# Routing attention and a top-1 router: four 32-row mask products side by side, and the preparation pieces gathered at one place per turn

## The chip, the cores and the metric

The kernel runs on one core of a Trainium2 chip. The metric is the time of one execution on the device in microseconds (us); the figure for a kernel is the median of several runs. Engines are named as in the profile: PE is TensorE (matmuls and transposes; PEld its weight loads), DVE is VectorE, ACT is ScalarE, POOL is GpSimd, SP is SyncE, which issues most DMAs.

## The reference

Attention with routing by clusters, then a router that sends each token to one of eight experts. Sizes: 4 batches, 8 heads, 768 rows, head width 64, 16 clusters; 3072 tokens of width 512, expert width 1024.

```python
q_assign = np.argmax(np.einsum('bhsd,hcd->bhsc', q_n, c_n), axis=-1)
k_assign = np.argmax(np.einsum('bhsd,hcd->bhsc', k_n, c_n), axis=-1)
mask = q_assign[:, :, :, None] == k_assign[:, :, None, :]
scores = scale * np.matmul(q, k.transpose(0, 1, 3, 2))
scores = np.where(mask, scores, -1000000000.0)
scores = scores - np.max(scores, axis=-1, keepdims=True)
attn = np.exp(scores)
attn = attn / (np.sum(attn, axis=-1, keepdims=True) + 1e-09)
return np.matmul(attn, v).astype(np.float32)
...
logits = xn @ en.T / tau
expert_idx = np.argmax(logits, axis=1)
...
    h = np.maximum(x[mask] @ w1[e], 0.0)
    out[mask] = gate_w[mask, None] * (h @ w2[e])
```

The token rows `x` of the router are the attention's output, heads side by side.

## The kernel before, in words

**Stages.** Attention, then a short stage that sorts tokens by expert, then 28 blocks of 128 tokens through their expert. The change is in the attention alone.

**Units, turns, pairs, groups.** Two heads are worked on together (a head pair; 16 of them, four per batch). A pair has 12 units: two halves of the query rows (`hq`, 384 each) by six tiles of 128 keys (`j`). Six units are a group, which has one output bank `o_ps`. The main loop takes two units a turn, so a pair has six turns (0 to 5) and a group three. In a turn it issues the scores and exponentials of the next two units, then the attends of its own two: the loop is one turn ahead with the scores.

**A unit.** `scores` (L338): per head one mask product in bf16 (64 rows of `kH` by `qH`, which hold one-hot cluster numbers times 2^60 and a -1/1 column, so that pairs in different clusters end at a huge negative value), then per head the f32 product of `kT` and `qT`, accumulated in the same banks `s_ps` (two banks a unit, two units at a time). The two heads lie on rows 0 to 63 and 64 to 127 of the array. `expo` (L349): ACT takes the exponential into `prob` (five buffers). `attend`: PE multiplies `prob` with `v` into `o_ps` (L358), two heads on two column halves; DVE adds `prob` into the running sum `acc` (L367 for a group's first two units, L377 for the others).

**End of a group.** One turn later, in turns 0 and 3: `total` sums `acc` over the partitions on PE (L385) and ACT copies it to `den` (L393); `divide` takes the reciprocal on DVE (L401) and makes `xT` (L402), with `ev`, a tiny multiple of the sum of the values. `rows` transposes `xT` on PE (L419) and ACT copies it to `xr` (L424), in turns 2 and 5.

**Preparation of the next pair** is cut in pieces, and `prep()` takes the next one at two places of a turn: between the scores and the attends, and behind the attends (and `total`, `divide`). The pieces in order: `turn` transposes the first halves of q and k (L220; ACT copies q, L227, DVE copies k, L229), with `values`, which sums v on POOL (L291 to L293); `turn` of q's second half; of k's; `products` with the centroids on PE (L235, copied by ACT, L243); `assign` (PE transposes, L248; DVE finds each row's maximum, L256, and where it is, L257; POOL multiplies by a preference, L258, so that ties go to the first); `choose` (DVE: L264 the best preference `pm`, L265 the one-hot `oh`); an empty one; `turn_hot` of q (six bf16 transposes on PE, L277, copied by DVE, L283); of k (six more, copied by ACT, L285); `mean` (L298, L306), which makes `ev`.

**Routing of a batch** (`route_pieces`) runs in the turns after its last group, one piece a turn at the end of a turn: `products` with the expert embeddings (L441, copy L449), `logits` (L454, L457), `norms` (three squares on ACT, L467), and `choose` (some 12 small DVE operations, L478 to L493, with a square root and an exponential on ACT, each with a table load), then the rows are written to DRAM. For the last batch these pieces come one after the other behind the loop.

**Buffers.** PSUM: four banks for scores, two for outputs, and two (`psM`, taken by `misc()` in turn) for everything else: each use waits until the one two before it has been copied out.

**Order.** PE, DVE and ACT issue in the order of the program text. POOL and SP are ordered by a scheduler. Loads of q, k, v of the next pair are issued on SP at a pair's start in the text; the first expert weights behind the loads of pair 2.

The loop's place for a piece, before:

```python
piece = prepare.pop(0) if prepare else None
```

Of the kernel before, what the change touches and what calls it, by code (L numbers as in the profile page):

```python
# [35 lines left out]
def kernel(  # L36
# [67 lines left out]
    with ExitStack() as at:  # L104
# [15 lines left out]
        def load(n):  # L120
            b, hp = pairs[n]
            t = ld[n] = {}
            for nm, src in (("q", q), ("k", k), ("v", v)):
                t[nm] = ldp.tile([P, NJ, 2, D], F32, tag=nm + "32", name=nm + "32")
                for h in range(2):
                    nc.sync.dma_start(
                        out=t[nm][:, :, h],
                        in_=src[b, 2 * hp + h].rearrange("(p j) d -> p j d", j=NJ),
                    )
# [4 lines left out]
        load(0)  # L134
# [34 lines left out]
        ohs = [const.tile([P, NJ // 2, 4, 2, D], BF16, name=f"oh{i}") for i in range(2)]  # L169
        for oh in ohs:  # L170
            nc.gpsimd.memset(oh, 0.0)
            for t in range(2):
                nc.gpsimd.memset(oh[:, :, 2 * t : 2 * t + 2, :, C : C + 1], (-1.0, 1.0)[t])
# [35 lines left out]
        def prep_pieces(n):  # L209
# [21 lines left out]
            def products():  # L231
# [10 lines left out]
                t["asT"] = smp.tile([P, HS], F32, tag="asT", name="asT")  # L242
                nc.scalar.copy(t["asT"], bk[:, 0:HS])  # L243

            def assign():
                bk = misc()
                for u in range(NJ // 2):
                    nc.tensor.transpose(  # L248
                        bk[:, P * u : P * u + P], t["asT"][:, P * u : P * u + P], ident
                    )  # L250
# [3 lines left out]
                sel = smp.tile(shp, BF16, tag="sel", name="sel")  # L254
# [5 lines left out]
            def choose():  # L260

                shp = [P, 4 * NJ, C]
                pm = smp.tile(shp[0:2], BF16, tag="pm", name="pm")
                nc.vector.tensor_reduce(pm, t["sel"], axis=AXX, op=ALU.max)  # L264
                nc.vector.tensor_tensor(  # L265
                    oh.rearrange("p u t h c -> p (u t h) c")[:, :, 0:C],
                    t["sel"],
                    bc(pm, shp, 2),
                    ALU.is_equal,
                )  # L270

            def turn_hot(i, nm):
                hot = t[nm + "H"] = trp.tile([P, S], BF16, tag=nm + "H", name=nm + "H")
                bk = misc().bitcast(BF16)
                for j in range(NJ):
                    half, u = divmod(j, NJ // 2)
                    nc.tensor.transpose(  # L277
                        bk[:, P * j : P * j + P],
                        oh[:, u, 2 * i + half].rearrange("p h c -> p (h c)"),
                        identb,  # L280
                    )
                if nm == "q":
                    nc.vector.tensor_scalar(hot, bk[:, 0:S], BIG, None, ALU.mult)  # L283
                else:
                    nc.scalar.copy(hot, bk[:, 0:S])  # L285
# [10 lines left out]
            def mean():  # L296
                bk = misc()
                nc.tensor.matmul(  # L298
                    bk[:, 0:1],
# [6 lines left out]
                nc.vector.tensor_copy(t["ev"], bk[:, 0:1])  # L306


            return [
                lambda: (turn("q", 0), turn("k", 0), values()),  # L310
                lambda: turn("q", 1),
                lambda: turn("k", 1),
                products,
                assign,
                choose,
                None,
                lambda: turn_hot(0, "q"),
                lambda: turn_hot(1, "k"),
                mean,
            ]  # L320

# [8 lines left out]
        def scores(i):  # L330

            n, hq, j = units[i]
            t = ld[n]
            s_ps = un[i]["s_ps"] = psS.tile([P, 2, 512], F32, tag="s_ps", name="s_ps")
            for l, r, first in (("kH", "qH", True), ("kT", "qT", False)):
                for h in range(2):
                    rows = slice(D * h, D * h + D)
                    nc.tensor.matmul(  # L338
                        s_ps[:, h, 0:HS],
                        lhsT=t[l][rows, P * j : P * j + P],  # L340
                        rhs=t[r][rows, HS * hq : HS * hq + HS],
                        start=first,
                        stop=not first,
                    )
# [84 lines left out]
        def route_pieces(b):  # L429
# [4 lines left out]
            def products(half):  # L434
# [13 lines left out]
                t["pT"] = smp.tile([P, HS], F32, tag="asT", name="asT")  # L448
                nc.scalar.copy(t["pT"], bk[:, 0:HS])  # L449

            def logits(half):
                bk = misc()
                for u in range(U):
                    nc.tensor.transpose(  # L454
                        bk[:, P * u : P * u + P], t["pT"][:, P * u : P * u + P], ident
# [8 lines left out]
            def norms(half):  # L464
                for j in range(U * half, U * half + U):
                    junk = smp.tile([P, DM], F32, tag="junk", name="junk")
                    nc.scalar.activation(  # L467
                        junk, xr[b][:, j, 0:DM], ACTF.Square, accum_out=t["sq"][:, j : j + 1]
                    )

            def choose():
# [26 lines left out]

            return [
                lambda: products(0),  # L500
                lambda: (logits(0), norms(0)),
                lambda: products(1),
                lambda: (logits(1), norms(1)),
                choose,
            ]


        prepare, routing = [], []

        def prep():  # L510
            piece = prepare.pop(0) if prepare else None
            if piece:
                piece()

        with tc.manual_schedule(engines={EngineType.PE, EngineType.DVE, EngineType.Activation}):
            for piece in prep_pieces(0):
                if piece:
                    piece()
            for m in range(2):
                scores(m)  # L520
                expo(m)


            for i in range(0, len(units) + 6, 2):
                g, part = divmod(i, GU)
                if i < len(units) and i % (2 * NJ) == 0:
                    n = i // (2 * NJ)
                    assert not prepare
                    if n + 1 < len(pairs):
                        load(n + 1)  # L530
                        prepare = prep_pieces(n + 1)
                    if n == 1:

                        for w in range(2):
                            nc.sync.dma_start(
                                out=w1s[w], in_=moe_w1[0].rearrange("(c p) f -> p c f", p=P)
                            )
                            nc.sync.dma_start(
                                out=w2s[w], in_=moe_w2[0].rearrange("(c p) d -> p c d", p=P)
                            )  # L540
                for m in range(i + 2, min(i + 4, len(units))):
                    scores(m)
                    expo(m)
                prep()
                if part == 4 and g > 0:
                    rows(g - 1)
                for m in range(i, min(i + 2, len(units))):
                    attend(m)
                if part == 0 and g > 0:
                    total(g - 1)  # L550
                    divide(g - 1)
                prep()
                if routing:
                    routing.pop(0)()
                if part == 4 and g > 0 and g % (2 * NHP) == 0:
                    assert not routing
                    routing = route_pieces(g // (2 * NHP) - 1)
            for piece in routing:
# [251 lines left out]
```

## Time and profile before

| | |
|---|---|
| median of 3 runs | 904.12 us (903.97 to 904.96) |
| the profiled execution | 904.4 us, its span 902.4 us, mean PE clock 0.973 |
| PE busy | 842.1 us (93%) |
| DVE, ACT, POOL busy | 357.1, 301.6, 127.8 us |
| L338, products of q and k, f32, x768 | 156.3 us busy, 486 ns each |
| L338, masks, bf16, x384 | 63.9 us busy, 329 ns each |
| L358, attends, f32, x768 | 145.1 us busy, 499 ns each |
| L377, sums on DVE, x128 | 130.1 us busy, 1017 ns each |
| L401, reciprocals on DVE, x32 | 81.7 us busy, 2552 ns each |
| L277, one-hot transposes, x192 | 16.7 us busy, 226 ns each |
| L258, POOL's product, x16 | 24.3 us busy, 1516 ns each |

The timeline has start, duration, engine, line, operation, names, shapes, count, and in brackets the idle time before it and what ended it. The rows of a stretch have: from and to; its length; busy time and count of PE, PEld, DVE, ACT, POOL; PE's granted clock; the DMA engines' busy share; GB/s. PE's matmuls overlap: a record lasts longer than the time until the next one starts. An f32 product shows as two records. The slices of the page are 22.6 us each.

### The profile page before, as it was taken

What the parts mean: (1) busy time and instruction counts of PE and PEld (TensorE: products, weight loads), DVE (VectorE), ACT (ScalarE), POOL (GpSimd) and SP (SyncE); (2) the same over time, 40 slices, a digit from 0 to 9 for tenths busy, and PEclk for the clock granted to TensorE, in tenths of its full rate; (3) what the DMA queues carried; (4) which work ended last, traced back from release to release, by engine and by line L of the source; (5) the groups of instructions that cost most, each with busy time, mean ns of one, the idle gap of its engine ahead of it and who ended that gap; (6) DMA issues with size and microseconds to landing.
All of it is one profiled execution on the core that took longest, in us unless ns stands there. A gap on an engine that the chain in (4) does not pass through costs nothing.

```text
span 902.4 us, 12774 instructions
## 1 busy us (share of the span) xinstructions
PE 842.1 (93%) x5207; PEld 495.4 (55%) x5207; DVE 357.1 (40%) x488; ACT 301.6 (33%) x485; POOL 127.8 (14%) x171
## 2 busy tenths in 40 slices
PE   4999999999999999999628999999999999999996
PEld 2444444444444444444216777767676777767672
DVE  3577777877777877687750000000000000000000
ACT  3545556654566555755330111111111111111110
POOL 4011010211111111110021011110101010101010
PEclk8999999999999999999957999999999999999998
DMA  9822211322213122020011380756565656405610
GB/s 246 303 54 53 53 36 35 108 53 53 53 36 106 36 54 53 19 88 1 1 70 36 117 321 26 259 188 256 192 259 188 259 196 260 156 24 198 234 36 21
DMA packets 105645, 106.85 MB, mean 118 GB/s; under 512 B 77157, under 2 KB 77157, under 8 KB 105072
## 3 DMA queue, kind: packets, MB, share of 16 engines
q1 hardware_dynamic: 100928, 92.30, 31.8%
q0 software_dynamic: 4480, 13.65, 4.0%
q8 instruction: 43, 0.70, 0.3%
q14 instruction: 18, 0.15, 0.0%
q10 hardware_dynamic: 176, 0.05, 0.0%
HBM read 152.11 MB, written 13.64 MB: 184 GB/s over the span
## 4 chain that ended last, share of the span: by engine, by line
PE 38%; issue 28%; DMA 20%; DVE 9%; ACT 2%; POOL 1%; SPq 0%; POOLq 0%; DVEq 0%
DMA out_dram<-y,sidx 19%; PE s_ps L338 15%; PE o_ps L358 12%; DVE den L401 4%; PE misc L220 3%; PE misc L385 2%; PE misc L235 2%; PE misc L419 1%; DVE acc L377 1%; DVE xT L402 1%; ACT den L393 1%; PE misc L441 1%; PE misc L248 1%; DVE qH L283 1%; PE misc L298 1%
## 5 line engine op out<-in xcount | busy, mean ns | idle before, releaser
L714 PEld LDWEIGHTS h_ps<-xTm,w1s 128*128 128x128 f32 x1792 | 204.6, 193 | 22.1 <-DVE xTm L704 19.7
L714 PE MATMUL h_ps<-xTm,w1s 128*128 128x128 f32 x1792 | 208.7, 278 | 2.9 <-DMA w1s<-in_moe_w_dram 2.9
L727 PE MATMUL y_ps<-w2s,hT 128*128 128x512 f32 x448 | 201.2, 592 | 0.0
L349 ACT ACTIVATE prob<-s_ps 128x768 f32<-128x768 f32 x192 | 153.2, 811 | 100.2 <-PE s_ps L338 78.0
L704 DVE COPY xTm<-x_ps 128x512 f32<-128x512 f32 x28 | 19.4, 691 | 380.9 <-PE x_ps L702 380.9
L338 PE MATMUL s_ps<-qT,kT 64*128 64x384 f32 x768 | 156.3, 486 | 0.0
L358 PE MATMUL o_ps<-prob,v 128*64 128x384 f32 x768 | 145.1, 499 | 0.0
L377 DVE TENSOR_TENSOR acc<-acc,prob 128x768 f32<-128x768 f32 x128 | 130.1, 1017 | 4.9
L727 PEld LDWEIGHTS y_ps<-w2s,hT 128*128 128x128 f32 x448 | 81.0, 190 | 81.3 <-issue 81.3
L721 ACT ACTIVATE hT<-h_ps 128x512 f32<-128x512 f32 x56 | 33.4, 597 | 243.7 <-PE h_ps L714 243.7
L401 DVE RECIPROCAL den<-den 128x384 f32<-128x384 f32 x32 | 81.7, 2552 | 30.8 <-ACT den L393 30.8
L338 PEld LDWEIGHTS s_ps<-qT,kT 64*128 64x128 f32 x768 | 69.3, 190 | 21.3 <-issue 21.3
L736 POOL DMA_INDIRECT out_dram<-y,sidx x28 | 28.5, 1017 | 356.1 <-ACT y L735 350.2
L358 PEld LDWEIGHTS o_ps<-prob,v 128*64 128x64 f32 x768 | 46.5, 136 | 56.7 <-issue 55.1
L338 PE MATMUL s_ps<-qH,kH 64*128 64x384 bf16 x384 | 63.9, 329 | 1.6 <-ACT prob L349 1.3
L735 ACT ACTIVATE y<-y_ps,xin 128x512 f32<-128x512 f32 x28 | 19.2, 687 | 136.1 <-PE y_ps L727 129.9
L291 POOL TENSOR_TENSOR vs<-v 128x384 f32<-128x384 f32 x16 | 17.0, 1063 | 220.5 <-DMA v<-in_v_dram 220.5
L338 PEld LDWEIGHTS <-kH 64*128 64x128 bf16 x384 | 19.4, 94 | 51.7 <-issue 37.0
L229 DVE COPY kT<-misc 128x384 f32<-128x384 f32 x32 | 17.7, 553 | 54.0 <-PE misc L220 54.0
L258 POOL TENSOR_TENSOR sel<-sel,prefc 128x384 bf16<-128x384 bf16 x16 | 24.3, 1516 | 103.5 <-DVE sel L257 103.5
L393 ACT COPY den<-misc 128x384 f32<-128x384 f32 x32 | 15.3, 479 | 50.4 <-PE misc L385 50.4
L674 POOL DMA_INDIRECT xin<-x_rows,gidx x28 | 29.0, 1035 | 12.3 <-issue 8.2
(146 smaller groups left out, 511.8 us busy)
## 6 DMA issues: line engine op xcount, KB each, us to landing
w1s<-in_moe_w_dram SPq DMA_DIRECT2D x30, 2048.0 KB
w2s<-in_moe_w_dram SPq DMA_DIRECT2D x30, 2048.0 KB
x_rows<-xr SPq DMA_DIRECT2D x4, 1539.0 KB
q<-in_q_dram SPq DMA_DIRECT2D x32, 192.0 KB
k<-in_k_dram SPq DMA_DIRECT2D x32, 192.0 KB
v<-in_v_dram SPq DMA_DIRECT2D x32, 192.0 KB
xin<-x_rows,gidx POOLq DMA_INDIRECT x28, 7.2
out_dram<-y,sidx POOLq DMA_INDIRECT x28, 7.1
```

The costliest lines, as they stand in the source:

```text
L220: nc.tensor.transpose(bk[:, P * j : P * j + P], t[nm][:, NJ // 2 * half + j].rearrange("p h d -> p (h d)"), ident,)
L338: nc.tensor.matmul(s_ps[:, h, 0:HS], lhsT=t[l][rows, P * j : P * j + P], rhs=t[r][rows, HS * hq : HS * hq + HS], start=first, stop=not first,)
L349: nc.scalar.activation(d["prob"], d["s_ps"][:, :, 0:HS], ACTF.Exp)
L358: nc.tensor.matmul(g["o_ps"][D * h : D * h + D, 0:HS], lhsT=ld[n]["v"][:, j, h], rhs=d["prob"][:, h], start=(j == 0), stop=(j == NJ - 1),)
L377: nc.vector.tensor_tensor(g["acc"], g["acc"], d["prob"], ALU.add)
L393: nc.scalar.copy(d["den"], bk[:, 0:HS])
L401: nc.vector.reciprocal(d["den"], d["den"])
L674: nc.gpsimd.indirect_dma_start(out=xin, out_offset=None, in_=x_rows[:], in_offset=bass.IndirectOffsetOnAxis(ap=gidx[:, j : j + 1], axis=0) ...
L714: nc.tensor.matmul(bk[:, m : m + P], lhsT=w1s[j % 2][:, c, f0 + m : f0 + m + P], rhs=d["xT"][:, P * c : P * c + P], start=(c == 0), stop=( ...
L721: nc.scalar.activation(d["hT"][:, f0 : f0 + 512], bk, ACTF.Relu)
L727: nc.tensor.matmul(bk, lhsT=d["hT"][:, P * c : P * c + P], rhs=w2s[j % 2][:, c], start=(c == 0), stop=(c == KF - 1),)
L736: nc.gpsimd.indirect_dma_start(out=out[:], out_offset=bass.IndirectOffsetOnAxis(ap=sidx[:, j : j + 1], axis=0), in_=y, in_offset=None, bou ...
```

## The change

- The one-hot tiles become 32 wide in place of 64 (`oh` has 2C columns per head). q's tiles are made twice, so that a q tile has the two heads on rows 0 to 63 and again on rows 64 to 127; k's tiles have an even and an odd `j` on the two halves, which makes three k tiles in place of six. `scores` takes two units at once: four mask products on rows 0, 32, 64 and 96, into four banks, then the four f32 products.
- `choose` follows `assign` at once, and writes its one-hots in three operations. `mean` writes into a column of the bank that holds the turned k one-hots.
- All pieces stand in `between`, after the scores and ahead of the attends: turn 5 the first halves of q and k of the pair after next; turn 0 the second halves of the next pair; turn 1 `values`, `products`, and `rows`; turn 2 `assign`, `choose`, and `rows`; turn 4 both `turn_hot` and `mean`. Routing: both products in turn 3 of the next batch's first pair, one norm a turn, both logits and `choose` in turn 3 of its second pair. At the end of the last batch the first half's routing stands ahead of the last rows.
- q and k are loaded two pairs ahead from turn 4, v one pair ahead from turn 0.

```diff
+        ohs = [const.tile([P, 3 * NJ, 2, 2 * C], BF16, name=f"oh{i}") for i in range(2)]
...
-                t["asT"] = smp.tile([P, HS], F32, tag="asT", name="asT")
+                t["asT"] = smp.tile([P, HS], F32, tag="asT", name="asT", bufs=1)
...
-                sel = smp.tile(shp, BF16, tag="sel", name="sel")
+                sel = smp.tile(shp, BF16, tag="sel", name="sel", bufs=1)
...
+                for r in range(2):
+                    nc.vector.tensor_tensor(
+                        qs[:, :, r],
+                        t["sel"][:, 0:G].rearrange("p (j h) c -> p j h c", h=2),
+                        bc(pm[:, 0:G].rearrange("p (j h) -> p j h", h=2), [P, NJ, 2, C], 3),
+                        ALU.is_equal,
+                    )
                 nc.vector.tensor_tensor(
...
+                    hots[:, 2], t["sel"][:, G:], bc(pm[:, G:], [P, G, C], 2), ALU.is_equal
+                )
...
+            def turn_hot_k():
+                hot = t["kH"] = trp.tile([P, HS], BF16, tag="kH", name="kH")
+                bank = misc()
+                bk = bank.bitcast(BF16)
+                for j in range(NJ // 2):
...
+                nc.scalar.copy(hot, bk[:, 0:HS])
+                mean(bank)
...
-            def mean():
-                bk = misc()
+            def mean(bk):
+
+                col = slice(HS, HS + 1)
                 nc.tensor.matmul(
-                    bk[:, 0:1],
+                    bk[:, col],
...
+            return {
+                "turn0": lambda: (turn("q", 0), turn("k", 0)),
+                "turn1": lambda: (turn("q", 1), turn("k", 1)),
+                "values": values,
+                "products": products,
+                "assign": lambda: (assign(), choose()),
+                "hots": lambda: (turn_hot_q(), turn_hot_k()),
+            }
...
         def scores(i):
...
+            for m in (i, i + 1):
+                un[m]["s_ps"] = psS.tile([P, 2, 512], F32, tag="s_ps", name="s_ps")
+            for m in (i, i + 1):
+                n, hq, j = units[m]
                 for h in range(2):
-                    rows = slice(D * h, D * h + D)
+                    r = D * (j % 2) + 2 * C * h
                     nc.tensor.matmul(
...
+                        un[m]["s_ps"][:, h, 0:HS],
+                        lhsT=ld[n]["kH"][r : r + 2 * C, P * (j // 2) : P * (j // 2) + P],
+                        rhs=ld[n]["qH"][r : r + 2 * C, HS * hq : HS * hq + HS],
+                        start=True,
+                        stop=False,
+                    )
+            for m in (i, i + 1):
...
+                        lhsT=ld[n]["kT"][D * h : D * h + D, P * j : P * j + P],
+                        rhs=ld[n]["qT"][D * h : D * h + D, HS * hq : HS * hq + HS],
+                        start=False,
+                        stop=True,
                     )
...
+        def piece(n, name):
+            if n < NP:
+                if n not in prepare:
+                    prepare[n] = prep_pieces(n)
+                prepare[n][name]()
+
+        def between(n, it):
+            b, nb = divmod(n, NHP)
+            if it == 5:
+                piece(n + 2, "turn0")
+                if n + 1 == NP:
+                    route[b] = route_pieces(b)
+                    rows(2 * n)
+                    route[b][0](0)
+            elif it == 0:
+                piece(n + 1, "turn1" if n else "turn0")
+            elif it == 1:
+                piece(n + 1, "values")
+                piece(n + 1, "products")
+                if n > 0:
+                    rows(2 * n - 2)
+            elif it == 2:
+                piece(n + 1, "assign")
+                if n > 0:
+                    rows(2 * n - 1)
+            elif it == 4:
+                piece(n + 1, "hots")
+            if b > 0:
+                if nb == 0 and it == 3:
+                    route[b - 1] = route_pieces(b - 1)
+                    for half in range(2):
+                        route[b - 1][0](half)
+                j = NJ * nb + it - 3
+                if 0 <= j < NJ:
+                    route[b - 1][2](j)
+                if nb == 1 and it == 3:
+                    for half in range(2):
+                        route[b - 1][1](half)
+                    route[b - 1][3]()
...
+            for i in range(0, len(units), 2):
+                n, it = divmod(i // 2, NJ)
+                if it == 0 and n + 1 < NP:
+                    load(n + 1, "v")
+                if it == 4 and n + 2 < NP:
+                    load(n + 2, "qk")
...
+                if i + 2 < len(units):
+                    scores(i + 2)
                 for m in range(i + 2, min(i + 4, len(units))):
-                    scores(m)
                     expo(m)
...
+                between(n, it)
+                for m in range(i, i + 2):
                     attend(m)
...
+                if i % GU == 0 and i > 0:
+                    total(i // GU - 1)
+                    divide(i // GU - 1)
+                if i == 0:
+                    piece(1, "turn1")
+            total(ngroups - 1)
+            divide(ngroups - 1)
+            products, logits, norms, choose = route[B - 1]
+            for j in range(NJ // 2):
+                norms(j)
+            logits(0)
+            rows(ngroups - 1)
+            products(1)
+            for j in range(NJ // 2, NJ):
+                norms(j)
+            logits(1)
+            choose()
```

## The prediction

> **What bounds the kernel.** I read the 40 slices and the busy times first, then the rows of stretches, then the timeline of PE turn by turn.
>
> ```profile
> span 902.4 us, 12774 instructions
> PE   4999999999999999999628999999999999999996
> DVE  3577777877777877687750000000000000000000
> 200.00:300.00 100.00, 97.60 (x660) 45.01 (x658) 75.61 (x95) 56.84 (x93) 13.84 (x21) 1.00 0.25 64
> 314.98:340.91 25.93, 25.52 (x173) 11.87 (x171) 19.67 (x22) 13.38 (x20) 3.47 (x4) 1.00 0.21 47
> ```
>
> The first 19 slices are the attention, the last 20 the expert blocks, which the change leaves alone. In attention PE is busy 97.6 of 100 us at clock 1.00; DVE follows with 75.6. The last row is one head pair (6 turns of two units): 25.93 us. Whatever takes PE's time there, or makes PE wait, is in the end. Two stretches of PE and one of DVE give the prices:
>
> ```profile
> 427.03 0.81 PE L338 MATMUL s_ps<-qT,kT 64*128 64x384 f32 x4
> 427.77 1.51 PE L358 MATMUL o_ps<-prob,v 128*64 128x384 f32 x8
> 429.21 0.34 PE L338 MATMUL s_ps<-qH,kH 64*128 64x384 bf16 x2
> ...
> 207.77 0.34 PE L338 MATMUL s_ps<-qH,kH 64*128 64x384 bf16 x2
> 207.94 0.81 PE L338 MATMUL s_ps<-qT,kT 64*128 64x384 f32 x4
> 208.59 0.33 PE L338 MATMUL s_ps<-qH,kH 64*128 64x384 bf16 x2
> 208.75 0.81 PE L338 MATMUL s_ps<-qT,kT 64*128 64x384 f32 x4
> 209.49 0.55 PE L220 MATMUL misc<-ident,q 128*128 128x128 f32 x3
> 209.87 0.49 PE L220 MATMUL misc<-ident,k 128*128 128x128 f32 x3
> 210.29 1.51 PE L358 MATMUL o_ps<-prob,v 128*64 128x384 f32 x8
> ...
> 327.63 0.56 DVE L257 TENSOR_TENSOR sel<-misc,amax 128x384 bf16<-128x384 f32 x1
> 328.11 2.53 DVE L377 TENSOR_TENSOR acc<-acc,prob 128x768 f32<-128x768 f32 x2
> 330.56 0.54 DVE L264 TENSOR_REDUCE pm<-sel 128x24 bf16<-128x384 bf16 x1
> ```
>
> Matmuls overlap, so starts count, not durations. Two masks side by side take 0.165 us (207.77 to 207.94, 208.59 to 208.75), the product of a unit 0.64 (207.94 to 208.59). Where the form of the tile changes there is more: 208.75 to 209.49 is 0.74, 0.10 over 0.64; the attend block takes 1.44 up to the masks (427.77 to 429.21), of which 4 x 0.32 = 1.28 is stream, 0.10 the change to the masks, and 0.05 its slower first step. From 208.75 to 210.29 there are 1.54, against 0.74 without an insertion (427.03 to 427.77): six f32 transposes at 0.11 make 0.66, so a stretch of pieces between two blocks costs about 0.15 beside its work.
>
> **Saved on PE, for each of 15 head pairs that prepare another.**
> - One of two mask steps a turn: 6 x 0.165 = 0.99, if four 32-row masks take as long as two of 64 rows do now. Bounds: 0.165 (all side by side) and 0.33 (two at a time, nothing saved). I take 0.165, the rows' own result for tiles side by side.
> - Stretches of pieces: nine a pair now (five before the attends, four behind). After it there are five places, one with two forms, so six: 3 x 0.15 = 0.45.
> - Three of twelve mask transposes, 0.057 each (six end 0.34 after they start): 0.17.
> - The products block now takes 1.0 because it waits for the kT copy of the same turn; a turn later it needs 0.64 and its 0.15, so 0.22 less.
> - The mean's present wait for qH, 0.41 (idle before L298 at 311.08; its cover, a second bank, is shared away).
> Sum 2.24.
>
> **Added for each pair.**
> - A change of form inside the scores, 32 rows to 64. No row shows 32-row tiles. Every change that the trace has, in rows or columns, costs 0.09 to 0.10, and with f32 weights behind it 0.05 more. I take 0.14, six times: 0.84. Bounds: 0 (mask to product within the 64-row form now) and 0.24 (the product's weight load of 190 ns, unhidden, and the 0.05).
> The Trainium skill, "TensorEngine Tiling (Array Packing)", section Key Properties, speaks against this edit: changing the tiling mode drains the array, while another tile of one mode does not. The 0.10 at 209.49 is this case's size of such a drain; by the rule without a size one could only say that the gain shrinks. "TensorE: Matmul & The Clock Gate", Part 3, gives 3.07 for four 32-row tiles rather than 4; by that the four masks would take some 0.215, and an estimate by that page adds 96 x 0.05, some 5 us, to the sum: 914 in place of 909.
> - The wait for the sums. Now DVE goes from sel straight to the two accs, and pm and oh (331.13 in the timeline) come behind them; POOL's product hides under the accs. After it `choose` stands before the accs of turn 2: POOL's product is waited for (0.91 with DVE idle, 15.82 in the timeline; 1.55 beside the accs), then pm 0.54, then three smaller one-hot operations instead of one. These are 192 wide; between 0.21 for 48 and 0.57 for 384 I estimate 0.33 each. From the start of turn 2: scores done 1.55, transposes 2.05, amax 2.25, sel to 3.4, POOL to 4.4, pm to 5.0, one-hots to 6.0, accs to 7.9. `total` of turn 3 needs the second; PE comes to it at 3.9 + 1.65 + 1.43 = 7.0, and the signal takes 0.12. So PE stands 1.1 us; all behind it (total, the next scores, the exponentials) is later by that. Bounds 0.7 and 1.5 (one-hots at 0.25; POOL at 1.55).
> - The wait of `mean`. It now writes into the bank that ACT copies kH out of, and ACT has the two exponentials of the turn ahead. From the start of turn 4: exponentials begin at 1.1 and 1.9 and end at 2.7, the copy (half as wide, 0.48) at 3.1, mean at 3.2; the transposes ended at 2.2. So 0.95, with the attends behind it. If mean needn't wait, the masks of turn 5 wait instead: total's delay puts the reciprocal (2.55), xT (0.62) and qH (0.55) to 13.2 after turn 2 began, and the masks would come at 12.6. So 0.6 to 1.1. The Trainium skill, "PSUM — Partial Sum Buffer", section on bank collisions, says that two engines mustn't use one bank at once; no row here shows it tried.
> Sum 2.89; net +0.65, times 15: **+9.8 us**.
>
> **Other moves.** Routing: the two pairs with a batch's routing take 55.33 now (126.49 to 181.82), 3.47 over two plain pairs. After it, both products stand in one place of turn 3 (2 x 0.64 + 0.15 = 1.43) and cover the 1.1 of total: +0.3. The logits (0.81) cover 0.8 of the other. But `choose` of the routing stands before turn 3's acc on DVE, with two table loads of 1.28 on ACT between its parts: the acc comes at 7.3 after the turn's start, exponential, kH copy, mean and then qH follow late, which I put at 2.4. Together +2.4 instead of 3.47: **-3** for three batches (bounds -6 and +3).
>
> End: products, copy and logits of the first half and three norms now stand behind the last rows. The products of the halves start at 450.35 and 453.29, so this is 2.94 on the way to `eq`, and the square root moves as much:
>
> ```profile
> 444.70 0.87 PE L385 MATMUL misc<-acc,ones 128*64 128x384 f32 x4 [2.09 <-DVE acc L377]
> 449.55 0.87 PE L419 MATMUL misc<-ident,xT 128*128 128x128 f32 x3 [3.98 <-DVE xT L402]
> 450.35 1.51 PE L441 MATMUL misc<-xT,embT 128*32 128x384 f32 x8
> 453.29 1.51 PE L441 MATMUL misc<-xT,embT 128*32 128x384 f32 x8
> ```
>
> They move into PE's gaps of 2.09 and 3.98, and the norms under the reciprocal: **-2.9**. Were the gaps gone, it would be 0.
>
> Start: two more one-hot operations and mean behind the kH copy, less three transposes: **+0.5**.
>
> Loads: q and k of the pair after next leave SP where they do now in time (their buffers are free after the transposes); v follows a pair's end and lands some 5.6 later (issued 315.15, summed from 320.78), so POOL has vs by turn 2 and its product is not behind it. The expert weights (8 MB early) are over by slice 2; pair 3 is transposed at about 70 us. All at nothing, hidden by 10 us or more; an uncovered load would cost its landing, about 5, once. One asT and one sel instead of two are free a pair ahead: nothing.
>
> Sum: 904.4 of the profiled execution (span 902.4 and 2.0 around it) + 9.8 - 3 - 2.9 + 0.5 = 908.8; the median of before is 0.3 under that execution. **Forecast 909**, its own range 903 to 917.
>
> **Rivals.**
> - *The inner change of form is free.* All forms here have 128 columns and only the rows differ. For it: nothing stands between mask and product of 64 rows. Against: 128x128 to 64x128 (306.85 to 307.00 in the timeline) has the 0.09 too. Price: 96 x 0.14 = 13.4 less, **895.5**, faster. It decides from 0.07 us a change downward.
> - *The masks don't run four at a time*: 96 x 0.165 = 15.8 more, **925**. For it: four f32 products on 32 columns do run together (0.64 for a routing half), so tiles of 32 work on columns; rows are not shown.
> - *Mean doesn't wait for the copy* (other columns of the bank): 15 x 0.35 = 5 less, **904**.
> - *The sums aren't waited for* (DVE ahead enough): 15 x 1.1 less, **892**. Against it: DVE's list above.
> That four masks are not issued as said is excluded by the row numbers r = 0, 32, 64, 96.
>
> **Chances.** Forecast 0.52, free change 0.22, masks in twos 0.11, mean 0.10, sums 0.05. What a measurement can tell is 0.2%, 902.3 to 905.9. Faster: 0.22 + 0.05 + 0.03 of mean = 0.30; same: 0.07 of the forecast + 0.04 = 0.11; slower 0.59. The range goes from 895 to 922: it holds the free change and what bounds the forecast's terms, and leaves most of the masks in twos out.
>
> **What would show it.** Mask to first product: 0.30 and not 0.16. `total` of turn 3 with an idle time near 1 us put down to acc, and mean one near 1 us put down to kH. DVE idle some 1 us before pm. PE's sum in a plain pair without waits near 24.5, the pair 26.6. `eq` 2.9 us nearer to the last attends. I am wrong if total starts without waiting, or if the step from masks to products shows no more than its stream.

## The result, and the profile after

| | before | after |
|---|---|---|
| median, on the same chip | 904.05 us (903.87 to 904.96, 4 runs) | 917.92 us (916.62 to 919.57, 4 runs) |
| ratio, 95% interval | | 1.0152 [1.0134, 1.0171] |
| profiled execution, its span | 904.4, 902.4 | 918.43, 916.4 |
| a pair that prepares another, no routing | 25.95 | 27.00 |

The changed kernel is 13.9 us slower; the forecast was 5 us. The direction and the two new waits came as foretold, the size did not. First the page of the changed kernel (its span, and PE, DVE and PE's clock in 40 slices), then the row of one pair, columns as before:

```profile
span 916.4 us, 12694 instructions
...
PE   4999999989999999989934999999999999999996
...
DVE  3477677677677667676663000000000000000000
...
PEclk8899999999999999999965999999999999999998
```

```profile
330.08:357.08 27.00, 25.38 (x170) 11.34 (x170) 19.57 (x25) 12.51 (x20) 2.82 (x4) 1.00 0.21 45
```

PE's busy time in a pair has barely moved (25.52 before, 25.38 now), but the pair is 1.07 longer than the one shown before: PE now stands 1.62 us in it, where it stood 0.41. The DVE digits of the attention have fallen from 7 and 8 to 6 and 7: DVE too does the same in a longer time. PE's timeline shows where it stands, in turns 3 and 4 of that pair (start, duration, what, and in brackets the idle time and what ended it):

```profile
343.21 0.34 PE L354 MATMUL s_ps<-qH,kH 32*128 32x384 bf16 x4
343.48 1.56 PE L364 MATMUL s_ps<-qT,kT 64*128 64x384 f32 x8
344.97 1.51 PE L384 MATMUL o_ps<-prob,v 128*64 128x384 f32 x8
347.28 0.87 PE L411 MATMUL misc<-acc,ones 128*64 128x384 f32 x4 [0.80 <-DVE acc L403]
348.08 0.34 PE L354 MATMUL s_ps<-qH,kH 32*128 32x384 bf16 x4
348.35 1.56 PE L364 MATMUL s_ps<-qT,kT 64*128 64x384 f32 x8
349.85 0.51 PE L287 MATMUL misc<-identb,oh 128*128 128x128 bf16 x6
350.19 0.33 PE L299 MATMUL misc<-identb,oh 128*128 128x128 bf16 x3
351.34 0.35 PE L319 MATMUL misc<-epsc,vs 128*128 128x1 f32 x2 [0.82 <-ACT kH L304]
```

Three readings. The four masks form one group of 0.34 us, about as long as one mask alone (329 ns before): they do run side by side. From the masks to the first product there are 0.27 (343.21 to 343.48) where two masks took 0.165. And two waits stand where none stood: `total` for the sums (0.80 idle; the last attend step starts at 346.00 and streams for 0.32, so 0.96 are lost), and `mean` for ACT's copy of kH out of its own bank (0.82 idle; 0.98 after the transposes' end, 350.36). DVE in turn 2 shows why the sums are late:

```profile
342.14 0.56 DVE L259 TENSOR_TENSOR sel<-misc,amax 128x384 bf16<-128x384 f32 x1
343.72 0.55 DVE L266 TENSOR_REDUCE pm<-sel 128x24 bf16<-128x384 bf16 x1 [1.02 <-POOL sel L260]
344.31 0.63 DVE L271 TENSOR_TENSOR oh<-sel,pm 128x192 bf16<-128x192 bf16 x2
344.85 0.35 DVE L277 TENSOR_TENSOR oh<-sel,pm 128x192 bf16<-128x192 bf16 x1
345.12 2.02 DVE L403 TENSOR_TENSOR acc<-acc,prob 128x768 f32<-128x768 f32 x2
```

DVE waits 1.02 for POOL and does `choose`, and only then the two accs, whose second ends as `total` starts. In the view of waits (us in total, times, longest), `mean`'s wait and DVE's wait for POOL stand once for each of the 16 pairs prepared. `total`'s wait stands ten times: in the nine pairs without routing, 0.8 each (1.0 in the first), and once at the end of attention. In the six pairs with routing, the routing's products and logits fill PE's time there.

```profile
PE misc L319 <- ACT kH L304: 17.0, 16, 2.2
PE misc L411 <- DVE acc L403: 8.7, 10, 1.3
DVE pm L266 <- POOL sel L260: 16.4, 16, 1.0
```

**The whole difference of the spans, 14.0 us, by place.** Each row is the difference between the two traces of one stretch.

| stretch | forecast | measured |
|---|---|---|
| start, up to the first attend (26.41, now 29.78) | +0.5 | +3.4 |
| 15 preparing pairs, a plain one 25.95, now 27.00 | +9.8 | +15.8 |
| what three batches' routing adds over plain pairs (3.44 each; now 2.53, 3.63, 3.85) | -3.0 | -0.3 |
| end, from the last pair's first attend to `eq` (33.81, now 31.44) | -2.9 | -2.4 |
| `eq` to the end: sorting and expert blocks | 0 | -2.5 |
| sum | +4.4 | +14.0 |

### The profile page after: what moved, and what is told of

The parts are those of the page before. It is cut to its first block, busy times and chain, and to the rows that moved or that the text cites. A ratio compares the mean times of both kernels' runs of the same rounds, so it can differ in the third digit from the quotient of the medians.

```text
span 916.4 us, 12694 instructions
## 1 busy us (share of the span) xinstructions
PE 843.0 (92%) x5159; PEld 489.9 (53%) x5159; DVE 356.5 (39%) x520; ACT 288.7 (32%) x485; POOL 116.1 (13%) x171
## 4 chain that ended last, share of the span: by engine, by line
PE 36%; issue 29%; DMA 19%; DVE 9%; ACT 3%; POOL 2%; SPq 0%; POOLq 0%; DVEq 0%; ACTq 0%
DMA out_dram<-y,sidx 19%; PE s_ps L364 13%; PE o_ps L384 11%; PE misc L223 3%; PE s_ps L354 2%; DVE acc L403 2%; PE misc L411 2%; ACT prob L375 2%; POOL sel L260 1%; PE misc L238 1%; DVE den L427 1%; PE misc L445 1%; DVE oh L271 1%; DVE pm L266 1%; PE misc L252 1%
## 5 line engine op out<-in xcount | busy, mean ns | idle before, releaser
L375 ACT ACTIVATE prob<-s_ps 128x768 f32<-128x768 f32 x192 | 147.5, 809 | 180.8 <-PE s_ps L364 139.3
L364 PE MATMUL s_ps<-qT,kT 64*128 64x384 f32 x768 | 154.1, 521 | 0.0
L403 DVE TENSOR_TENSOR acc<-acc,prob 128x768 f32<-128x768 f32 x128 | 122.0, 953 | 3.7
L354 PEld LDWEIGHTS <-kH 32*128 32x128 bf16 x384 | 10.0, 91 | 59.1 <-issue 59.1
L354 PE MATMUL s_ps<-qH,kH 32*128 32x384 bf16 x384 | 33.9, 338 | 1.3 <-DVE qH L292 0.8
L411 PE MATMUL misc<-acc,ones 128*64 128x384 f32 x128 | 26.7, 494 | 8.9 <-DVE acc L403 8.7
L393 DVE SCALAR_TENSOR_TENSOR acc<-prob 128x768 f32<-128x768 f32 x32 | 30.3, 946 | 0.0
```

The lines of the kernel that those rows point to most:

```text
L354: nc.tensor.matmul(un[m]["s_ps"][:, h, 0:HS], lhsT=ld[n]["kH"][r : r + 2 * C, P * (j // 2) : P * (j // 2) + P], rhs=ld[n]["qH"][r : r + 2 ...
L364: nc.tensor.matmul(un[m]["s_ps"][:, h, 0:HS], lhsT=ld[n]["kT"][D * h : D * h + D, P * j : P * j + P], rhs=ld[n]["qT"][D * h : D * h + D, H ...
L375: nc.scalar.activation(d["prob"], d["s_ps"][:, :, 0:HS], ACTF.Exp)
L393: nc.vector.scalar_tensor_tensor(out=g["acc"], in0=un[i - 1]["prob"], scalar=NJ * EPS, in1=d["prob"], op0=ALU.add, op1=ALU.add,)
L403: nc.vector.tensor_tensor(g["acc"], g["acc"], d["prob"], ALU.add)
L411: nc.tensor.matmul(bk[D * h : D * h + D, 0:HS], lhsT=ones, rhs=d["acc"][:, h], start=True, stop=True,)
```

## The experiments

The ratios are against the kernel before, with the 95% interval; each set of runs on a chip had its own runs of that kernel (904.09, 904.19 and 903.88 us).

**1. Four masks or two, in the new form.** Is the step of 0.27 from the masks to the products the price of four masks at a time, or of the change of rows? Only the order of the changed kernel's scores is altered: each unit has its two masks and at once its own products, so the rows change four times a turn in place of two.

```diff
             for m in (i, i + 1):
                 n, hq, j = units[m]
                 for h in range(2):
...
                         lhsT=ld[n]["kH"][r : r + 2 * C, P * (j // 2) : P * (j // 2) + P],
...
-            for m in (i, i + 1):
-                n, hq, j = units[m]
                 for h in range(2):
...
                         lhsT=ld[n]["kT"][D * h : D * h + D, P * j : P * j + P],
```

> The changed kernel with the 32-row masks issued unit by unit (two masks, two products, two masks, two products), so that the change of form from 32 to 64 rows comes twice a turn and not once. Theory (the change of form costs 0.22 us: 0.11 ahead of the first product, 0.11 in its first step): a turn gains a mask step of 0.165, a change back of 0.10 and a change forth of 0.22, 0.485 in all, 95 turns, +46 us: 964. Rival (four masks side by side are slow themselves, 0.27, and only the 0.11 in the first product is the change): two masks take 0.165 again, so a turn gains about 0.27, +26 us: 943. Rival (changes of form are free and the step is something else): +0.165 a turn, 934.

Measured: 950.89 (950.31 to 951.62), 1.0521 [1.0503, 1.0538]. PE's timeline of this kernel, one turn's scores:

```profile
334.38 0.34 PE L354 MATMUL s_ps<-qH,kH 32*128 32x384 bf16 x2
334.64 0.92 PE L362 MATMUL s_ps<-qT,kT 64*128 64x384 f32 x4
335.49 0.34 PE L354 MATMUL s_ps<-qH,kH 32*128 32x384 bf16 x2
335.76 0.92 PE L362 MATMUL s_ps<-qT,kT 64*128 64x384 f32 x4
336.60 0.55 PE L252 MATMUL misc<-ident,asT 128*128 128x128 f32 x3
```

Two masks take the same 0.26 to 0.27 up to the products as four do, so four are not slower than two, and 0.10 of it goes with the change of rows. And the products take 0.85 up to the next change (334.64 to 335.49), two steps of 0.32 in the 64-row form and 0.21 more: 0.11 for the first step, which is 0.43 in the trace's single records, and 0.10 for the change back. The changed kernel has the same: its products take 1.49 (343.48 to 344.97), four steps of 0.32, the 0.11 and the 0.10 of the change to the attends, which stood there before too. So four masks side by side add 0.10 ahead of the products and 0.11 in them, 0.21 a turn.

PE's weight loads (PEld) show what stands behind this. One turn's masks and the products behind them, in the kernel before and in the one after:

```profile
315.00 0.10 PEld L338 LDWEIGHTS <-kH 64*128 64x128 bf16 x2 [0.60 <-issue]
315.01 0.36 PEld L338 LDWEIGHTS s_ps<-qT,kT 64*128 64x128 f32 x4
```

```profile
343.21 0.10 PEld L354 LDWEIGHTS <-kH 32*128 32x128 bf16 x4 [0.60 <-issue]
343.48 0.95 PEld L364 LDWEIGHTS s_ps<-qT,kT 64*128 64x128 f32 x8 [0.17 <-issue]
```

With 64-row masks the products' weights begin to load 0.01 behind the masks' own, while the masks run, and the product follows at 315.18. With 32-row masks they begin to load only at 343.48, with the first product itself, and that product is the slow one. So the load (187 ns in the median) is no longer hidden. That the 0.11 is this load is the likely reading; no run takes the two parts apart, and none issues 32-row masks one behind the other without a change of rows.

The time came out 13 us below what the theory gave. Some 6 of it are PE's shorter waits, because a slower PE waits less for the same work: 4.6 in all for the sums and 15.1 for kH, where the changed kernel has 8.7 and 17.0. The plain turn grew by 0.46 (0.485 expected), the turn with `total`'s wait became shorter, 6.65 to 6.59. The step's price holds; the kernel's total can't be had by multiplying it.

**2. `choose` behind the attends of turn 2.** It leaves `assign` where it is and takes the wait for POOL, pm and the one-hots out from in front of the accs.

```diff
-                "assign": lambda: (assign(), choose()),
+                "assign": assign,
+                "choose": choose,
...
+                if it == 2:
+                    piece(n + 1, "choose")
```

> The changed kernel with choose (pm and the one-hots on DVE) behind the attends of turn 2, so that the sums do not wait for POOL. Theory: the wait of total in turn 3, 0.97 us a pair, goes and nothing takes its place: plain pair 27.0 to 26.0, 15 pairs, -14.5 us: 903. Rival (DVE has no slack, the wait only moves to the qH copy and the masks of turn 5): plain pair at 26.6 or more, 912 to 918.

Measured: 905.48 (902.07 to 905.9), 1.0009 [0.9999, 1.0019]; a pair takes 25.98. PE of this kernel in turns 3 and 4:

```profile
334.67 1.51 PE L385 MATMUL o_ps<-prob,v 128*64 128x384 f32 x8
336.01 0.82 PE L412 MATMUL misc<-acc,ones 128*64 128x384 f32 x4
...
340.02 0.35 PE L319 MATMUL misc<-epsc,vs 128*128 128x1 f32 x2 [0.82 <-ACT kH L304]
```

`total` starts 1.34 after the attends, with no idle time, where it took 2.31. `mean` waits as before. On DVE the accs stand ahead of pm again:

```profile
332.31 2.53 DVE L404 TENSOR_TENSOR acc<-acc,prob 128x768 f32<-128x768 f32 x2
334.76 0.54 DVE L266 TENSOR_REDUCE pm<-sel 128x24 bf16<-128x384 bf16 x1
```

So the wait of `total` was the place of `choose`, and it was worth 1.02 a pair.

**3. `mean` ahead of the copy.** It writes into the same bank, but before ACT reads it; only then is kH copied, and DVE's copy of `ev` comes last.

```diff
-                nc.scalar.copy(hot, bk[:, 0:HS])
                 mean(bank)
+                nc.scalar.copy(hot, bk[:, 0:HS])
+                ev(bank)
```

> The changed kernel with the matmul of mean issued ahead of ACT's copy of kH, in the same bank. Theory: mean's wait of 0.98 us goes, but as total is still late, qH (behind the reciprocal on DVE) comes late for the masks of turn 5, which wait about 0.6: plain pair 26.6, -6 us: 912. Rival (nothing takes the wait's place): plain pair 26.0, 903.

Measured: 910.03 (909.0 to 913.24), 1.0077 [1.0053, 1.0101]; a pair takes 26.43. PE of this kernel, turn 4:

```profile
341.60 0.33 PE L299 MATMUL misc<-identb,oh 128*128 128x128 bf16 x3
341.77 0.33 PE L320 MATMUL misc<-epsc,vs 128*128 128x1 f32 x2
342.04 1.51 PE L387 MATMUL o_ps<-prob,v 128*64 128x384 f32 x8
343.91 0.34 PE L357 MATMUL s_ps<-qH,kH 32*128 32x384 bf16 x4 [0.36 <-DVE qH L292]
```

`mean` follows the transposes at once: the wait was for the copy out of the shared bank. Some 0.4 of the 1.0 comes back in the next masks, which wait for qH, as the prediction's working had it for the case that `mean` needn't wait. So 0.57 a pair is gained.

**4. The masks alone.** The kernel before, pieces and places as they were, with 32-row one-hots in three operations and the four masks side by side.

```diff
-                lambda: turn_hot(0, "q"),
-                lambda: turn_hot(1, "k"),
+                turn_hot_q,
+                turn_hot_k,
...
-                for m in range(i + 2, min(i + 4, len(units))):
-                    scores(m)
-                    expo(m)
+                if i + 2 < len(units):
+                    scores(i + 2)
+                for m in range(i + 2, min(i + 4, len(units))):
+                    expo(m)
```

> The kernel before with nothing changed but the masks: 32-row one-hots, four masks side by side, scores of two units at once; all pieces where they were. Theory (the change of form costs 0.22): a turn loses a mask step of 0.165 and gains 0.22, +0.05 x 96 = +5, and three transposes fewer a pair, -2.7: 906. The forecast's price (0.14): -2.4 - 2.7 = 899. Rival (the change of form is free): 96 x 0.165 + 2.7 = 18.5 less: 885.5.

Measured: 906.62 (905.91 to 907.68), 1.0030 [1.0020, 1.0041]. A pair takes 26.12 against 25.95, and `eq` comes at 462.49 against 457.77; the expert blocks give 2.8 back. Of the 4.7 at `eq`, 1.5 arise before the first attend; a turn with neither pieces nor waits takes 3.21 instead of 3.16, the 0.05 of the theory. That the total came so near the 906 is partly luck: the theory had neither the start nor the blocks. At the forecast's price of 0.14 this kernel would have been about 899 and without a price 885.5: both are excluded, and so is the pair that they would give, 25.6 and 24.8. Four masks side by side are no gain here.

**5. The new places with masks of 64 rows.** Experiment 3 with the one-hots, transposes and scores of the kernel before.

```diff
-            for m in (i, i + 1):
-                for h in range(2):
-                    r = D * (j % 2) + 2 * C * h
...
+                for l, r, first in (("kH", "qH", True), ("kT", "qT", False)):
+                    for h in range(2):
+                        rows = slice(D * h, D * h + D)
```

> The kernel with mean ahead of the copy, and its masks back in 64 rows, two at a time, unit by unit; all pieces stay at one place a turn. Theory (a change of form costs 0.21 or more and eats the mask step of 0.165): six turns gain 0.05 each, three transposes more cost 0.17, so the plain pair goes from 26.43 to about 26.3: 908. Rival (the four masks side by side bring something that the trace of the changed kernel hides): plain pair 26.7 or more, 914.

Measured: 903.54 (902.16 to 906.28), 0.9996 [0.9984, 1.0009]; a pair takes 25.92, where 26.3 was expected, and the total is 4.5 below the 908. A plain turn is 3.97 instead of 4.01, as expected. The rest of the gain was not: with one one-hot operation instead of three, DVE is earlier, and the turn with `total`'s wait is 5.48 instead of 5.65, the one that waits for qH 4.28 instead of 4.44. The three smaller operations cost through the wait too.

**6. Both waits taken away**, masks of 32 rows: the edits of experiments 2 and 3 together.

```diff
+                "choose": choose,
...
                 mean(bank)
+                nc.scalar.copy(hot, bk[:, 0:HS])
+                ev(bank)
...
+                if it == 2:
+                    piece(n + 1, "choose")
```

> The changed kernel with choose behind the attends and mean ahead of the copy, 32-row masks kept. Theory (the two waits are separate, and the masks' wait for qH shrinks as total comes on time): PE's work without waits is 27.0 - 0.97 - 0.98 = 25.05 a pair, with up to 0.35 left of the wait for qH, so 25.1 to 25.4, and 918 - 15 x 1.75 = 892. Rival (DVE's queue is full, so the waits come back elsewhere): plain pair 25.9 or more, 902.

Measured: 896.63 (896.17 to 897.47), 0.9923 [0.9906, 0.9939]: faster than before by 0.8%. A pair takes 25.42; qH is still waited for, as PE's timeline of this kernel shows behind the attends of turn 4:

```profile
335.60 0.34 PE L358 MATMUL s_ps<-qH,kH 32*128 32x384 bf16 x4 [0.38 <-DVE qH L292]
```

The total is 4.6 above what was expected: the second pair of each batch's routing, 27.67 in the kernel before, still takes 28.1 to 29.7. The gathered places are a gain as such, and the two waits took it all away.

**7 and 8. All places without waits**, once with masks of 64 rows and once of 32. Beside experiment 6: ACT copies qH, routing's `choose` goes behind the attends of turn 5, and the first transposes of the second pair stand ahead of the second scores.

```diff
-                nc.vector.tensor_scalar(hot, bk[:, 0:S], BIG, None, ALU.mult)
+                nc.scalar.activation(hot, bk[:, 0:S], ACTF.Copy, scale=BIG)
...
-                    route[b - 1][3]()
...
+                if it == 5 and n % NHP == 1 and n > NHP:
+                    route[n // NHP - 1][3]()
...
+            piece(1, "turn0")
             for i in range(0, len(units), 2):
```

> All pieces at one place a turn, but masks in 64 rows, choose behind the attends, mean ahead of the copy, qH copied by ACT, the routing's choose behind the attends of turn 5, and the first transposes of pair 1 ahead of the second scores. Theory: no wait is left, plain pair 25.05 - 0.30 + 0.17 = 24.9 against 25.95 before, 15 pairs, -16; end -3: 885 to 887. Rival (the gain of gathering the pieces is itself an error of the sum): 895 or more.

> The same as gathered_64rows with the 32-row masks of the change. Theory: 0.13 a pair slower than with 64 rows, plain pair 25.05, 2 us more: 887 to 889. Rival (32 rows bring a gain where nothing waits): 2 us or more faster than with 64 rows.

Measured: 64 rows 883.45 (882.78 to 884.1), 0.9774 [0.9758, 0.9790]; 32 rows 882.18 (881.9 to 883.84), 0.9766 [0.9750, 0.9782]. Both beat the kernel before by 2.3%, and so the changed one as well; the two aren't told apart, where the 32 rows were expected 2 us behind. PE in the one with 32 rows, end of turn 4, turn 5 and the next pair's turn 0:

```profile
323.62 0.34 PE L320 MATMUL misc<-epsc,vs 128*128 128x1 f32 x2
323.88 1.51 PE L388 MATMUL o_ps<-prob,v 128*64 128x384 f32 x8
325.33 0.34 PE L358 MATMUL s_ps<-qH,kH 32*128 32x384 bf16 x4
325.60 1.56 PE L368 MATMUL s_ps<-qT,kT 64*128 64x384 f32 x8
327.09 0.55 PE L223 MATMUL misc<-ident,q 128*128 128x128 f32 x3
...
331.91 1.51 PE L388 MATMUL o_ps<-prob,v 128*64 128x384 f32 x8
333.25 0.82 PE L415 MATMUL misc<-acc,ones 128*64 128x384 f32 x4
333.99 0.34 PE L358 MATMUL s_ps<-qH,kH 32*128 32x384 bf16 x4
```

and in the one with 64 rows, one turn's scores:

```profile
324.50 0.34 PE L344 MATMUL s_ps<-qH,kH 64*128 64x384 bf16 x2
...
326.21 0.55 PE L223 MATMUL misc<-ident,q 128*128 128x128 f32 x3
```

No bracket is left in the first: masks, `mean` and `total` start without idle time. From the masks to the pieces behind them there are 1.76 with 32 rows (325.33 to 327.09) and 1.71 with 64 (324.50 to 326.21): four masks side by side lose 0.05 a turn. Over a pair that is 0.3, less the three transposes of 0.057 that the 32-row one-hots save: 0.13 reckoned, 24.98 against 24.89 measured. Up to `eq` 32 rows are 1.3 us behind (439.27, 437.95), in the expert blocks 2.9 ahead (411.73, 414.61), 2.1 of it in the waits that the next experiments are about. What each of the three further edits is worth by itself wasn't tried.

**9 and 10. Why are the expert blocks shorter?** The group of PE's first expert product, with its idle time and what ended it, in the kernel before and in the one after:

```profile
L714 PE MATMUL h_ps<-xTm,w1s 128*128 128x128 f32 x1792 | 208.7, 278 | 2.9 <-DMA w1s<-in_moe_w_dram 2.9
```

```profile
L772 PE MATMUL h_ps<-xTm,w1s 128*128 128x128 f32 x1792 | 209.0, 278 | 0.5 <-DMA w1s<-in_moe_w_dram 0.5
```

In this group the kernel before and experiments 5 and 7, all with 64-row one-hots, wait 2.9, 4.0 and 2.5 for expert weights, at the changes of expert; the others, with 32 rows, 0.2 to 0.9. The 32-row tiles are smaller by 1536 bytes of each partition, so what is allocated behind them lies elsewhere in memory. Experiments 9 and 10 put a spare tile into experiment 8, of that size and of half of it (384 in place of 768):

```diff
+        spare = const.tile([P, 768], BF16, name="spare")
+        nc.gpsimd.memset(spare, 0.0)
```

> gathered_32rows with a spare tile of 1536 bytes a partition in the pool of constants, which is by how much the 32-row one-hots made that pool smaller; the tiles of the expert blocks then lie where they lie in the kernel before. What is asked is the 2.5 us by which the expert blocks are shorter in all kernels with 32-row masks. Theory (it is where the blocks' tiles lie): first transposes of the blocks to the last product 414.5 or more in place of 411.7, six waits on w1s in place of one, 885. Rival (it is the code or the order of the attention): 411.7 and 882 as without the tile.

> The same with half the spare tile, 768 bytes. Theory (place): the expert blocks' stage differs from both, or is like one of them: 411.7 to 414.6. Rival (code or order): 411.7.

Measured: full size 882.5 (881.96 to 883.89), 0.9760 [0.9743, 0.9776], wait 0.9; half 882.07 in one run, wait 0.4. The blocks' stage took 413.70 and 412.53, between the 411.7 and the 414.5 that were set against each other. But with the full tile there is one wait and not six, and the clock explains most of the rest: in the stage's first 8 us it was 0.50, where without the tile it was 0.71, some 1.6 us of full clock. So the place in memory, tried in this way, isn't it. What makes the loads come late with 64-row one-hots stays open.

## Why the prediction was right and wrong

**Wrong in size: the change of form inside the scores.** The step "a change of form inside the scores, 32 rows to 64", taken at 0.14, is the term that failed most. Experiment 1 has 0.10 for the change and 0.11 for the first f32 product behind it, 0.21 to 0.22, near the upper bound of 0.24. Six times a pair that is 1.29 in place of 0.84, so 0.45 more, and over 15 pairs **+6.7 of the 9.6** that the sum was short. PE's time in a plain pair without the two waits, put near 24.5, is 25.06 (27.00 less 0.96 and 0.98). The value taken was 0.10 for the change and 0.05 for the first step, from the attends; the products' first step is dearer by twice that. The upper bound had the case that the runs show: the product's weight load unhidden, as PEld's rows of experiment 1 have it. (The 15 pairs missed by 6.0 in all: small gains in the other terms made up the rest.) With 0.21 against a saving of 0.165, the masks side by side, the first half of the change, lose 0.05 a turn, and experiments 4, 7 and 8 show it.

The Trainium skill, "TensorEngine Tiling (Array Packing)", section Key Properties, says that a change of tiling mode drains the array; the runs agree, and give its size. By "TensorE: Matmul & The Clock Gate", Part 3, four 32-row tiles take longer than one, some 0.215 by the estimate in the prediction; here the step to the products is the same for two masks and for four, so no run shows that cost.

**Right.** The two waits: `total` 0.96 where 1.1 was put, `mean` 0.98 where 0.95 was, and experiments 2 and 3 take away each by the cause named. The sums' list on DVE with POOL's 0.91 in it, and DVE idle 1.02 before pm. The masks four at a time, and the products without their wait. The end: from the last masks to `eq` there are 18.16 where there were 21.11, the 2.95 foretold. With the form's true price the sum of a pair is 2.24 saved and 1.29 + 0.96 + 0.98 = 3.23 added, net +0.99, against 1.05 measured.

**Wrong: routing, put at -3, came out at -0.3** (+2.7). `choose` of the routing stands before turn 3's acc, and what follows is late, as the working says: `mean` waits 2.17 instead of 0.82. PE of the changed kernel, turn 4 of such a pair:

```profile
293.25 0.33 PE L299 MATMUL misc<-identb,oh 128*128 128x128 bf16 x3
295.75 0.35 PE L319 MATMUL misc<-epsc,vs 128*128 128x1 f32 x2 [2.17 <-ACT kH L304]
```

Then the clock is lower for the next stretch (PE's granted clock is the third figure from the end):

```profile
296.00:300.00 4.00, 4.00 (x17) 1.51 (x19) 3.77 (x6) 0.00 (x0) 0.00 (x0) 0.57 0.49 201
```

A wait of 2.17 in sparse work, and PE at about half speed until 299.8; in another batch the same from 409.0 to 412.4. That is not in the working. The first batch has the same wait of 2.17, at 185.23, but no low clock behind it, and adds 2.53 where the working had 2.4; the two with the low clock add 3.63 and 3.85. So the order of the pieces cost what was reckoned, and 2.4 of the 2.7 go with the low clock. Why it came in two places of three isn't shown. Experiments 7 and 8 moved `choose` behind the attends together with other things; alone it wasn't tried.

**Wrong: the start, put at +0.5, is +3.4** (+2.9). Paired scores make the second masks wait for both exponentials, and the clock is low for longer. PE's row from 20 to 30 us, of the kernel after:

```profile
20.00:30.00 10.00, 9.27 (x34) 4.54 (x36) 0.27 (x2) 5.13 (x7) 0.00 (x0) 0.50 1.04 398
```

and of the kernel before:

```profile
20.00:30.00 10.00, 9.66 (x55) 4.99 (x55) 1.58 (x3) 6.55 (x9) 0.00 (x0) 0.83 1.04 398
```

PE works as long, at 0.50 instead of 0.83, and does less. Experiment 3 tells the two apart. Its start is that of the changed kernel but for `mean`, and its clock is nearly that of the kernel before:

```profile
20.00:30.00 10.00, 8.79 (x49) 4.03 (x49) 1.77 (x5) 5.75 (x8) 0.00 (x0) 0.80 1.04 398
```

Its first attend comes at 27.50, so some 1.1 of the 3.4 are the change's own, where 0.5 was put, and the other 2.3 go with the low clock of this one execution. The other kernels with paired scores lie between, at 27.6 to 29.0. Another order of the start alone wasn't tried.

**Not foreseen: -2.5 in the expert blocks**, which the change leaves alone. 2.4 of it are shorter waits for expert weights (2.9 before, 0.5 now); why they are shorter is open (experiments 9 and 10). By luck it covers somewhat less than half of the two terms above. Without it the forecast would have been further off.

**The rivals.** That the change of form is free is excluded by experiments 1 and 4; masks in twos by the four in 0.34; `mean` and the sums without waits by the brackets. The forecast's case held, at a higher price.

## What to carry to other kernels

Packing more small tiles side by side pays only if the step saved (here 0.165) is longer than what the change of rows costs (here 0.21, half of it the dearer first step behind the change, whose weights no longer load ahead); measure that in the form that follows, not in another. When pieces are gathered at one place, look on each engine's queue for what now stands ahead of the work that the bottleneck waits for, and write into a shared bank before another engine reads it: with both done, the same gathering went from 1.5% slower to 0.8% faster, and with the three further edits of experiments 7 and 8 to 2.3% faster. A saving on PE that leaves its waits as they are can be lost in them, and a loss can be partly covered by them, so a term times its count is only sure in turns without a wait.

## What was not expected of the hardware

- From 64 bf16 rows to 64 f32 rows nothing stands between; from 32 rows to 64 there are 0.10 and a first f32 product of 0.43 instead of 0.32, and 0.10 on the way back where the next work follows, the same for two masks and for four. The product's weights load under the masks in the first case (315.01, product at 315.18) and only with the product in the second (343.48).
- POOL's product of 128x384 took 0.91 with DVE idle (342.77 in the timeline) and 1.52 on average before, beside DVE's sums.
- A wait of 2.17 on PE amid sparse work was followed by some 3.4 us at half clock, in two of three batches.
- Loads of expert weights arrive 0.2 to 1.1 us late at the changes of expert with 64-row one-hots and hardly with 32, in a stage that uses no one-hots. A spare tile of the same size doesn't bring it back.
